# Splitting the first weight load of a decode kernel: one half row per partition ahead of four and four

## The chip, the cores and the metric

The kernel runs on one core of a Trainium2 chip. The metric is the device time of one execution in microseconds (us). A profiled execution gives, beside its time, a span: the time from the first to the last instruction that the hardware profiler recorded.

## What is computed

One token `x` of width 576 is normalised, and two branches are computed from it and added to it: attention over the last 4096 positions of a key and value cache (32 query heads on 16 key and value heads of width 128), and a gated MLP with 4608 hidden values. Cut to what matters here:

```
xn  = layernorm(x)                                   # x: 576
q   = xn @ wq                                        # wq: 576 x 4096
p   = softmax(q . k_cache[last 4096] * 128 ** -0.5)  # two query heads on each of 16 key heads
A   = (p @ v_cache[last 4096]) @ wo                  # wo: 4096 x 576
z   = gelu(xn @ w_in)                                # w_in: 576 x 4608
B   = (z[:2304] * (w_sp * layernorm(z[2304:]) + b_sp)) @ w_out
out = x + A + B
```

All inputs are bf16. The weights and the two caches together are 50.96 MB, and each byte is read once.

## The kernel before

All large transfers are issued from one queue, SyncE's (SP), in program order: the query weights `wq`, two loads of keys, the MLP's `w_in` in three loads, then keys and values by turns, the last values, `w_out`, and `wo` in four loads of 16, 10, 4 and 2 rows per partition. Each load takes one buffer of a ring of seven equal buffers (`RING = 7`, tag "ring"). A load can be issued only when what its buffer held seven loads earlier has been used; SP waits for that, and all later loads stand behind it. Each load also takes one of eight completion semaphores in turn, together with the four small transfers of ScalarE's queue, and waits until the transfer that had the semaphore before has landed.

`wq` is laid out so that partition p holds nine half rows of 2048 values (4096 B each), s = 0 to 8. `load_halves` (L76 to L81, issue on L80) loads a stretch of them for all 128 partitions in one DMA. The before kernel calls it twice for `wq`: five half rows, then four. In the trace a DMA on this queue shows as 128 packets, one for each partition (256 for keys and values, 8192 B each), spread over 16 DMA engines, and each DMA engine ends its part with a 4-byte packet for the semaphore.

ScalarE's queue carries four tiny transfers: `x64` (L110, the token on 64 partitions), `x4` (L113) and two single values (L116, L117).

The start of the computation is a chain: `x64` lands; one matmul spreads it (L174); VectorE, TensorE and GpSimd compute the mean and variance (L177 to L190); VectorE writes `XT` (L196 to L199); TensorE multiplies it with `wq` (L207: for each half row s, four matmuls of 512 columns side by side, accumulated in `qps`). Then `q_rep` (L216, L218), sixteen small matmuls (L224) and sixteen small multiplications on VectorE (L235) give `Qb`, the query operand of all heads. From there a loop goes over the 16 heads: VectorE transposes the keys (`t_head`, L247), TensorE computes the scores (`s_head`, L255), and after each group of four heads come the softmax and the product with the values (L276 to L305). The `w_in` product (L334) stands after the fourth head on TensorE. At the end TensorE multiplies with `w_out` and `wo` (L403, four matmuls a row), VectorE adds `x` (L425), and SP writes the result (L426).

Instructions of each engine run in program order (`tc.manual_schedule()`).

Of the kernel before, what the change touches and what calls it, by code (L numbers as in the profile page):

```python
# [39 lines left out]
def kernel(  # L40
# [31 lines left out]
    def ring_tile(name, rows, width):  # L72
        t = ring.tile([P, SLOT], BF16, name=name, tag="ring")
        return t[:, 0:rows * width].rearrange("p (s c) -> p s c", c=width)

    def load_halves(src, lo, n, name):  # L76

        v = ring_tile(f"{name}{lo}", n, src.shape[1] // 2)
        rows = src.rearrange("r (e c) -> (r e) c", e=2).rearrange("(p s) c -> p s c", s=NS)
        nc.sync.dma_start(v, rows[:, lo:lo + n, :])  # L80
        return [(lo + s, v[:, s, :]) for s in range(n)]  # L81
# [9 lines left out]
        return [(lo + t, v[:, t, :]) for t in range(n)]  # L91

    K, V = {}, {}
    wq_sb = load_halves(A_wq, 0, 5, "wq") + load_halves(A_wq, 5, 4, "wq")
    for m in range(2):
        K.update(load_kv(A_k_cache, m, "k"))
    win_sb = sum((load_halves(B_w_in, lo, 3, "win") for lo in (0, 3, 6)), [])
# [360 lines left out]
```

## Time and profile before

| | |
|---|---|
| median of 3 runs | 128.71 us (128.63 to 128.98) |
| the profiled execution: its time | 128.68 us |
| the profiled execution: its span | 126.9 us (1.78 us lie around it) |
| busy: TensorE matmuls, VectorE, ScalarE, GpSimd | 56%, 58%, 18%, 3% of the span |
| read from HBM | 50.96 MB, 402 GB/s over the span |
| 16 DMA engines, queue of the large loads | 95.2% of their span |
| TensorE's granted clock, mean | 0.781 |

In the timeline's lines the first two numbers are the start and the length in us, then come engine (SPq and ACTq are the DMA queues' issuing instructions), line, operation, output<-input and count, and in brackets the idle time before and what ended it. In the table of stages, "DMA share" is the time of all packets that started in the stage, as a share of 16 engines' time there (a long packet counts whole where it starts, so a short stage can show more than 1).

### The profile page before, as it was taken

Reading aid. Unit: us, or ns where it says so; the run is one execution under the profiler, and the core shown is the slowest. Engines: PE = TensorE matmul, PEld = TensorE weight load, DVE = VectorE, ACT = ScalarE, POOL = GpSimd, SP = SyncE. Lnnn points to the kernel's source line nnn. Section 1 sums busy time; section 2 is a strip of 40 time slices with the busy share of each in tenths; the row PEclk is TensorE's granted clock in tenths of the full one; section 3 lists DMA queues with packets and bytes.
Section 4 is the critical chain, followed back from the end, with each engine's and each line's share of the span. In section 5 each row is a group of like instructions: output and inputs, shape, how many; then the busy total and the mean of one; then the engine's idle time right before and its main releaser. Section 6 shows DMA issues by size and latency. Waiting matters only on the chain.

```text
span 126.9 us, 1775 instructions
## 1 busy us (share of the span) xinstructions
PE 70.5 (56%) x708; PEld 32.5 (26%) x708; DVE 74.1 (58%) x157; ACT 22.9 (18%) x76; POOL 3.6 (3%) x19
## 2 busy tenths in 40 slices
PE   0002831399999796008359456991579901862460
PEld 0002301132699621002113111231113301222350
DVE  6704145999000499455399799997999557050000
ACT  0300011000000003930000308303074039200000
POOL 3401000000000000000100000000000000000000
PEclk9999996579985559955868976999555996589755
DMA  4999999999999999999999999999999999999940
GB/s 136 433 409 429 408 429 434 444 436 418 427 413 431 418 426 429 421 431 434 421 436 423 424 436 423 429 424 421 429 431 423 431 452 442 427 418 413 415 171 0
DMA packets 5899, 51.06 MB, mean 402 GB/s; under 512 B 516, under 2 KB 516, under 8 KB 772
## 3 DMA queue, kind: packets, MB, share of 16 engines
q1 hardware_dynamic: 5800, 50.96, 95.2%
q8 instruction: 5, 0.08, 0.2%
q10 hardware_dynamic: 92, 0.00, 0.0%
q14 instruction: 2, 0.02, 0.0%
HBM read 50.96 MB, written 0.00 MB: 402 GB/s over the span
## 4 chain that ended last, share of the span: by engine, by line
issue 41%; DVE 27%; DMA 25%; PE 3%; POOLq 0%; POOL 0%
DMA wo<-in_A_wo_dram 18%; DVE kT L247 16%; DMA x<-in_A_x_dram 7%; PE out_t L403 2%; DVE mx L276 2%; DVE pt L288 2%; DVE on L319 2%; DVE om L315 1%; PE yps L322 1%; PE ps_x L184 0%; POOLq L453 0%; POOL mv L190 0%; DVE mt L265 0%; DVE lb L271 0%; DVE mb L271 0%
## 5 line engine op out<-in xcount | busy, mean ns | idle before, releaser
L255 PE MATMUL S<-kT,Qb 128*8 128x512 bf16 x128 | 40.5, 484 | 21.8 <-DVE kT L247 21.0
L247 DVE STREAM_TRANSPOSE kT<-k 128x1024 f32<-128x1024 f32 x32 | 37.0, 1211 | 10.8 <-DMA k<-in_A_k_cache_dram 10.8
L255 PEld LDWEIGHTS <-Qb 128*8 128x8 bf16 x128 | 11.7, 98 | 46.7 <-issue 38.5
L297 ACT COPY PT<-pt 32x32 f32<-32x32 f32 x64 | 15.4, 241 | 13.7 <-DVE pt L288 12.9
L281 ACT ACTIVATE p<-S,nm 128x1024 bf16<-128x1024 f32 x4 | 4.5, 1113 | 54.8 <-DVE nm L279 54.8
L305 PE MATMUL ops<-v,PT 128*8 128x512 bf16 x128 | 13.3, 453 | 0.4 <-ACT PT L297 0.4
L334 PEld LDWEIGHTS <-win 128*128 128x128 bf16 x162 | 10.1, 164 | 0.4 <-issue 0.4
L334 PE MATMUL zps<-XT,win 128*128 128x2 bf16 x162 | 10.2, 202 | 0.0
L322 PE MATMUL yps<-on,sel 128*32 128x32 f32 x32 | 2.1, 220 | 10.8 <-DVE on L319 10.8
L403 PE MATMUL out_t<-wo,Y 128*1 128x144 bf16 x128 | 3.7, 276 | 5.2 <-DMA wo<-in_A_wo_dram 5.2
L276 DVE TENSOR_REDUCE mx<-S 128x1 f32<-128x1024 f32 x4 | 4.8, 1204 | 1.6 <-PE S L255 1.6
L425 DVE TENSOR_TENSOR res<-out_t,x 97x144 bf16<-97x144 f32 x1 | 0.3, 308 | 9.1 <-PE out_t L403 9.1
L288 DVE STREAM_TRANSPOSE pt<-p 128x1024 bf16<-128x1024 bf16 x4 | 4.8, 1210 | 1.4 <-ACT p L281 1.4
L305 PEld LDWEIGHTS <-PT 128*8 128x8 bf16 x128 | 4.0, 91 | 5.8 <-issue 2.0
L174 PE MATMUL ps_x<-x,rmat 64*128 64x9 bf16 x1 | 0.2, 163 | 9.5 <-DMA x<-in_A_x_dram 9.5
L315 DVE SCALAR_TENSOR_TENSOR om<-ops,rs,dmask 128x512 f32<-128x512 f32 x4 | 3.0, 742 | 4.2 <-PE ops L305 4.2
L322 PEld LDWEIGHTS yps<-on,sel 128*32 128x32 f32 x32 | 1.7, 132 | 12.5 <-DVE on L319 10.4
L403 PEld LDWEIGHTS <-Y 128*1 128x1 bf16 x128 | 2.9, 97 | 6.0 <-issue 5.9
L207 PE MATMUL qps<-wq,XT 128*2 128x512 bf16 x36 | 3.8, 603 | 0.8 <-DVE XT L198 0.8
L319 DVE TENSOR_REDUCE on<-om 128x128 f32<-128x512 f32 x4 | 4.1, 1023 | 0.1
L218 DVE CAST q_rep<-qps 128x512 bf16<-128x512 f32 x2 | 1.4, 692 | 4.4 <-PE qps L207 3.7
L216 ACT CAST q_rep<-qps 128x512 bf16<-128x512 f32 x2 | 1.2, 585 | 14.2 <-DVE q_rep L218 14.2
(88 smaller groups left out, 35.0 us busy)
## 6 DMA issues: line engine op xcount, KB each, us to landing
k<-in_A_k_cache_dram SPq DMA_DIRECT2D x8, 2048.0 KB, 24.9
v<-in_A_v_cache_dram SPq DMA_DIRECT2D x8, 2048.0 KB, 21.7
win<-in_B_w_in_dram SPq DMA_DIRECT2D x3, 1728.0 KB, 20.6
wout<-in_B_w_out_dram SPq DMA_DIRECT2D x1, 2592.0 KB, 27.4
wq<-in_A_wq_dram SPq DMA_DIRECT2D x1, 2560.0 KB, 8.8
wo<-in_A_wo_dram SPq DMA_DIRECT2D x1, 2304.0 KB
wq<-in_A_wq_dram SPq DMA_DIRECT2D x1, 2048.0 KB, 13.0
wo<-in_A_wo_dram SPq DMA_DIRECT2D x1, 1440.0 KB
```

The costliest lines, as they stand in the source:

```text
L247: nc.vector.transpose(dst[:, 1024 * hf:1024 * (hf + 1)], src[:, 1024 * hf:1024 * (hf + 1)])
L255: nc.tensor.matmul(S[g % 2][32 * i:32 * i + 8, hf, :], lhsT=Qb[:, j, be].rearrange("p a h -> p (a h)"), rhs=kv[:, be // 2, be % 2, 16 * hf ...
L276: nc.vector.tensor_reduce(out=mx[:, 0:1], in_=s[:], op=ALU.max, axis=mybir.AxisListType.XY)
L281: nc.scalar.activation(p[:], s[:].rearrange("p a n -> p (a n)"), ACT.Exp, bias=nm[:, 0:1], scale=SCALE, accum_out=lx[:, 0:1])
L288: nc.vector.transpose(pt[:].rearrange("p t x -> p (t x)"), d["p"][:])
L297: nc.scalar.copy(PT4[32 * a:32 * a + 32, i, :], pt4[32 * i:32 * i + 32, :, a])
L305: nc.tensor.matmul(ops[32 * i:32 * i + 8, :], lhsT=d["PT"][:, i, 4 * tb:4 * tb + 4, :].rearrange("p t h -> p (t h)"), rhs=V[GK * g + i][:, ...
L315: nc.vector.scalar_tensor_tensor(out=om[:].rearrange("p c d -> p (c d)"), in0=ops[:], scalar=d["rs"][:, 0:1], in1=dmask[:].rearrange("p c ...
L319: nc.vector.reduce_sum(on[:], om[:].rearrange("p c d -> p d c"), axis=AXX)
L322: nc.tensor.matmul(yps[32 * g:32 * g + 32, :], lhsT=sel[:, dq, :], rhs=on[:, 32 * dq:32 * dq + 32], start=(dq == 0), stop=(dq == 3), tile_ ...
L334: nc.tensor.matmul(zps[:, :, t], lhsT=wt[:, t, :], rhs=XT[:, s, :], start=(s == 0 and t == 0), stop=(s == NS - 1 and t == NF - 1), skip_gr ...
L403: nc.tensor.matmul(out_t[32 * n:32 * n + 1, :], lhsT=lhs[:, col:col + 1], rhs=wv[:, CW * n:CW * (n + 1)], start=first, stop=last, tile_pos ...
```

## The change

`wq` is loaded in three DMAs of 1, 4 and 4 half rows per partition instead of two of 5 and 4. The first DMA then moves 128 x 4096 B, the second 128 x 16384 B, the third is as it was. The ring hands out one more buffer, so that the loads behind `wq` take the next buffer of the seven, and the next of the eight semaphores. The matmuls, their order and everything else in the program text are unchanged.

```diff
-    wq_sb = load_halves(A_wq, 0, 5, "wq") + load_halves(A_wq, 5, 4, "wq")
+    wq_sb = load_halves(A_wq, 0, 1, "wq") + load_halves(A_wq, 1, 4, "wq") + load_halves(A_wq, 5, 4, "wq")
```

## The prediction, made before the changed kernel was run

> **What bounds the kernel now.** I read first the slices of the page, then the chain that ended last, then the stages around the change, and last the issues of the transfers.
>
> The slices (40 of 3.17 us each), DMA engines and rate:
>
> ```profile
> DMA  4999999999999999999999999999999999999940
> GB/s 136 433 409 429 408 429 434 444 436 418 427 413 431 418 426 429 421 431 434 421 436 423 424 436 423 429 424 421 429 431 423 431 452 442 427 418 413 415 171 0
> ```
>
> From the second slice to the last but two, the DMA engines are never short of work. The chain that ended last agrees at its end:
>
> ```profile
> 98.10 23.38 DMA wo<-in_A_wo_dram
> 121.48 0.04 issue
> 121.52 1.37 PE out_t L403 x30
> ```
>
> A `wo` load issued at 98.10 lands 23.38 us later though it is 1440 KB, some 3.4 us at 430 GB/s: it stood some 20 us in the queue. After it only 5.4 us of span remain. So the time is start of the stream + bytes at the stream's rate + a fixed tail, as long as the queue never runs dry. The list of issues says that it doesn't:
>
> ```profile
> k<-in_A_k_cache_dram SPq DMA_DIRECT2D x8, 2048.0 KB, 24.9
> v<-in_A_v_cache_dram SPq DMA_DIRECT2D x8, 2048.0 KB, 21.7
> ```
>
> The third number is us from issue to landing. 2048 KB is 4.9 us at 430 GB/s, so a load typically waits 17 to 20 us behind others. The smallest of the eight `v` is 19.4 us. Compute that frees a buffer a microsecond sooner or later moves only this waiting.
>
> Now the head, where the change is (timeline):
>
> ```profile
> 0.74 0.86 SPq L80 DMA_DIRECT2D wq<-in_A_wq_dram  x2
> 1.65 1.20 SPq L85 DMA_DIRECT2D k<-in_A_k_cache_dram  x2
> 9.43 1.29 SPq L80 DMA_DIRECT2D win<-in_B_w_in_dram  x3
> 9.55 0.16 PE L174 MATMUL ps_x<-x,rmat 64*128 64x9 bf16 x1 [9.55 <-DMA x<-in_A_x_dram]
> 13.17 3.79 PE L207 MATMUL qps<-wq,XT 128*2 128x512 bf16 x36 [0.77 <-DVE XT L198]
> 17.02 0.69 DVE L218 CAST q_rep<-qps 128x512 bf16<-128x512 f32 x1 [3.72 <-PE qps L207]
> 22.90 9.13 DVE L247 STREAM_TRANSPOSE kT<-k 128x1024 f32<-128x1024 f32 x8
> 42.85 2.37 DVE L247 STREAM_TRANSPOSE kT<-k 128x1024 f32<-128x1024 f32 x2 [10.82 <-DMA k<-in_A_k_cache_dram]
> ```
>
> The token lands at 9.4 us, `XT` is ready 3.6 us later, the q matmuls end at 17.0, the first eight key transposes end at 32.0. Then VectorE waits 10.82 us for the third key load. Whatever the head gains or loses up to that size ends here.
>
> **The change, part by part.**
>
> *One more DMA in the stream.* Bytes are the same. The trace's packet records give the usual time of a packet by size: 2304 B 93 ns, 4608 B 178, 8192 B 309, 16384 B 611, 20480 B 761, 4 B 9 ns. Between 4608 and 20480 B a byte costs 583/15872 = 0.0367 ns, and 8 to 9 ns per packet are left over; a 4096 B packet is then 159 ns. A row of 20480 B (761) becomes 159 + 611 = 770 ns: +9. Each DMA engine has eight of the rows, and one more semaphore packet of 9 ns: 8 x 9 + 9 = 81 ns. All DMA engines run in parallel, so the stream ends +0.08 us later. Nothing hides this, as the stream is the bound.
>
> *The cold start.* In stages of 0.5 us (the last two numbers of a line are DMA share and GB/s):
>
> ```profile
> 1.50:2.00 0.50, 0.00 (x0) 0.00 (x0) 0.45 (x1) 0.00 (x0) 0.15 (x1) 1.00 2.06 492
> 2.00:2.50 0.50, 0.00 (x0) 0.00 (x0) 0.50 (x2) 0.00 (x0) 0.00 (x0) 1.00 0.53 123
> 2.50:3.00 0.50, 0.00 (x0) 0.00 (x0) 0.49 (x4) 0.00 (x0) 0.04 (x1) 1.00 0.09 41
> 3.00:3.50 0.50, 0.00 (x0) 0.00 (x0) 0.29 (x1) 0.48 (x1) 0.50 (x1) 1.00 1.27 532
> ```
>
> (492 + 123 + 41) x 0.5 us = 328 KB is exactly one 20480 B row on each of 16 DMA engines, and (2.06 + 0.53 + 0.09) x 0.5 = 1.34 us is its mean time, against 0.76 later: 0.58 us are start-up. The trace has no cold 4 KB row. Bounds: if the 0.58 us is a delay ahead of the first byte, the small row takes 0.74 us and nothing changes (0); if a cold first packet takes 1.34 us whatever its size, 0.60 us more is lost (1.34 - 0.74). A gain is possible only from the spread below. I take 0: second rows ran at 778 to 789 ns, nearly the usual time, so reading ahead hides the delay for all but the first, and the 2304 B packets at the end run at a steady 93 ns.
>
> *What starts earlier.* In the records `x64`'s 18-byte packets start at 5.34 us, after four `wq` rows on their DMA engine, then take turns with rows: four and a semaphore packet, ending 8.41 to 9.23 us. With 4 KB rows the same count of turns gives first packets near 3 us and landing near 4.3; if they come at 5.34 by time, five turns with 16 KB rows of 0.61 us end near 8.8. So `x` lands 0.6 to 5 us earlier, `XT` at 8 to 12.4. The second `wq` load lands where the first did (9.5), the third at 14.3 (before: issue 1.2 + 13.0 = 14.2, +0.08). Sixteen matmuls at 3.79/36 = 0.105 us stand behind the last, 1.7 us: q ends near 16.0, not 17.0. `Qb` and the first transposes start up to 1 us earlier. All of it goes into the 10.82 us wait: VectorE then waits 11.9 us for the third key load, which lands 0.08 later. Price 0; without that cover it would be -1.0.
>
> *Moved waits on SP.* The listing of the changed program against the old shows: the second key load now waits for `x64`'s semaphore (before, the first `w_in` load did), the next two for the first `wq` load and `x4`, and the third `w_in` load for the first single value and, new, for TensorE's four matmuls on half row 0, whose buffer it takes. All later loads are queued behind it on SP. Latest issue: the second key load 8.8 us, the third `w_in` load 12.8 us. Already queued then: 6.8 MB, which end at 2.4 + 15.9 = 18.3 us, and 12.4 MB, which end at 31 us. Cover 9 and 18 us, so price 0. The third key load still waits for `wq`'s matmuls: half rows 1 to 4, done before 15.5 as before. From the fourth key load on, each waits for the same work as before; the listing of TensorE, VectorE and ScalarE is the same but for one more wait (half row 1) and renumbered semaphores.
>
> *The tail* has the same loads in the same order: 0.
>
> Sum: 128.68 + 0.08 = 128.76, say 128.8 us. The profiled execution is 0.03 below the median of 128.71, far inside what a measurement of this kernel can tell from no change (0.3%, 0.39 us).
>
> The Trainium skill speaks against this change: "DMA: Bandwidth & Descriptors", Measured, asks for DMAs of 1 MiB or more, and its fit charges about 2 us for each DMA beside the bytes. The new first load has 0.5 MiB; by that rule taken at face value the sum would be near 130.8. The slices disagree: 26 loads in 122 us of steady 408 to 452 GB/s leave no room for 2 us each. No run here yet shows a small load at the head.
>
> **Rivals.**
>
> 1. *The cold start goes by packet* (slower). The first 4 KB row takes as long as the first 20 KB row, and the stream is 0.60 us behind for good: 128.76 + 0.60 = 129.4. It decides from 0.31 us of such loss on (0.39 less 0.08). For it: only one row per DMA engine moved up to 3 us. Against: the second rows' near-usual time. 0.13.
> 2. *A load's start isn't hidden* (slower). The small load is drained before the next is under way, so that a second start, issue to first packet (0.74 to 1.75 us) plus 0.58, 1.6 us, is paid: 130.4. Against: the second issue follows 0.46 us after the first, while the first row is still starting. 0.03. The skill's charge per DMA is this case.
> 3. *The earlier q counts* (faster). If the 10.82 us wait isn't the cover that I read, the 1.0 us comes through: 127.8. Against it: the queue's 17 to 20 us waits. 0.06.
> 4. *The late DMA engine shifts.* The slowest DMA engine sets the end. In the records their last packets of `wo` end between 121.3 and 123.2 us; 0.6 us of that spread is there after the first rows already (3.05 to 3.65), the rest comes from instruction fetches of 16 KB (0.9 us each) on the same engines. Shorter first rows may even out or reshuffle the 0.6: 128.2 or 129.3. 0.08 each way.
>
> That the change doesn't do what it says is out for the loads (the listing has three); that `x` isn't earlier would change nothing in the sum.
>
> **How the numbers follow.** Forecast, within 0.3%: 0.62, its own range 128.5 to 129.0 (runs of the old kernel lie within 0.35). Faster: rivals 3 and 4, 0.14. Slower: rivals 1, 2 and 4, 0.24. The range runs from the fast side of rival 4 to rival 1: 128.2 to 129.5, leaving out rivals 2 and 3.
>
> **What would show it.** Right: the first DMA packets of 4 KB at 159 ns, second rows at the usual time, 430 GB/s from 3 us on; `x` before 9 us; q matmuls in pieces, ending near 16.0; VectorE's wait for the third key load near 12 us and ending near 42.9; the last `wo` landings within 0.3 us of before. Wrong: a DMA share under 0.9 in a stage between 3 and 20 us (rivals 1, 2), the key wait gone (3), or the last `wo` landing moved by over 0.4 us with a full stream (4).

## The result, and the profile after

The changed kernel takes 128.87 us (median of 22 runs, 128.65 to 129.14) against 128.67 us of the kernel before (22 runs, 128.48 to 129.00): ratio 1.0016, 95% interval 1.0009 to 1.0022, so 0.12 to 0.28 us slower. That is within the 0.3% called no change, but it is more than the 0.08 us that the packets cost. The profiled execution took 128.82 us, with a span of 127.0 us.

The slices of the changed kernel:

```profile
DMA  4999999999999999999999999999999999999940
GB/s 84 438 434 439 400 426 428 439 427 440 440 399 423 431 416 428 428 431 431 423 426 434 423 426 434 423 423 426 428 434 423 423 467 433 409 449 399 420 180 0
```

The stream is as full as before. What differs is the first slice: 84 GB/s after 136. (Packets count where they start, and the rows started there are now small, so the drop is less than it looks.)

The issues still land some 20 us after they are made, so the queue never ran low:

```profile
k<-in_A_k_cache_dram SPq DMA_DIRECT2D x8, 2048.0 KB, 23.6
v<-in_A_v_cache_dram SPq DMA_DIRECT2D x8, 2048.0 KB, 22.0
```

The head in the timeline of the changed kernel:

```profile
0.74 1.33 SPq L80 DMA_DIRECT2D wq<-in_A_wq_dram  x3
...
4.87 0.16 PE L174 MATMUL ps_x<-x,rmat 64*128 64x9 bf16 x1 [4.87 <-DMA x<-in_A_x_dram]
5.17 5.12 SPq L80 DMA_DIRECT2D win<-in_B_w_in_dram  x3
...
9.32 2.30 PE L207 MATMUL qps<-wq,XT 128*2 128x512 bf16 x20
...
14.40 1.88 PE L207 MATMUL qps<-wq,XT 128*2 128x512 bf16 x16 [2.78 <-DMA wq<-in_A_wq_dram]
...
16.32 0.69 DVE L218 CAST q_rep<-qps 128x512 bf16<-128x512 f32 x1 [6.74 <-PE qps L207]
```

The token lands at 4.9 us instead of 9.4, the q matmuls run in two pieces, and q is done at 16.3 instead of 17.0. The 0.7 us won goes where the prediction sent it, VectorE's wait for the third key load (VectorE's timeline):

```profile
22.22 9.12 DVE L247 STREAM_TRANSPOSE kT<-k 128x1024 f32<-128x1024 f32 x8
42.76 2.37 DVE L247 STREAM_TRANSPOSE kT<-k 128x1024 f32<-128x1024 f32 x2 [11.42 <-DMA k<-in_A_k_cache_dram]
```

11.42 us of waiting instead of 10.82, ending within 0.1 us of where it ended. The chain that ended last goes through a `wo` load again, now the last of the four (before, the second, issued at 98.10):

```profile
101.51 22.13 DMA wo<-in_A_wo_dram
123.68 0.44 PE out_t L403 x8
124.14 0.31 DVE res L425
```

In the packet records the last `wo` packet ends at 123.18 us before and 123.32 now. The mean of the 16 DMA engines' ends, which is steadier than the last one, goes from 121.91 to 122.07 us.

The cold start in stages of 0.5 us (last two numbers: DMA share, GB/s):

```profile
1.50:2.00 0.50, 0.00 (x0) 0.00 (x0) 0.45 (x1) 0.00 (x0) 0.15 (x1) 1.00 0.99 90
2.00:2.50 0.50, 0.00 (x0) 0.00 (x0) 0.50 (x2) 0.00 (x0) 0.00 (x0) 1.00 0.64 106
2.50:3.00 0.50, 0.00 (x0) 0.00 (x0) 0.50 (x4) 0.00 (x0) 0.03 (x1) 1.00 0.72 213
3.00:3.50 0.50, 0.00 (x0) 0.00 (x0) 0.29 (x1) 0.49 (x1) 0.50 (x1) 1.00 0.94 360
```

(90 + 106 + 213) x 0.5 us = 205 KB started by 3 us are three rows of 4 KB on each of 16 DMA engines, in (0.99 + 0.64 + 0.72) x 0.5 = 1.2 us. In the running stream, three such rows take 3 x 0.159 = 0.48 us. So not only the first small row is slow. In the packet records 38 of the 128 small rows take over 15 ns longer than usual, the slowest 1.15 us.

To compare heads I add up, over the packets of the large loads in the first 7 us, the time beyond the usual one of their size (those over by more than 15 ns), and divide by 16. This start-up loss is 0.61 us for each DMA engine before and 0.76 in the changed kernel.

### The profile page after: what moved, and what is told of

Read it like the earlier page. It is cut to its first block, busy times and chain, and to the rows that moved or that the text cites. A ratio compares the mean times of both kernels' runs of the same rounds, so it can differ in the third digit from the quotient of the medians.

```text
span 127.0 us, 1776 instructions
## 1 busy us (share of the span) xinstructions
PE 70.9 (56%) x708; PEld 32.6 (26%) x708; DVE 74.1 (58%) x157; ACT 22.9 (18%) x76; POOL 3.7 (3%) x19
## 4 chain that ended last, share of the span: by engine, by line
issue 44%; DVE 28%; DMA 17%; PE 7%; POOLq 0%; POOL 0%; SPq 0%
DMA wo<-in_A_wo_dram 17%; DVE kT L247 14%; PE S L255 4%; DVE mx L276 2%; DVE pt L288 2%; DVE on L319 2%; DVE S L159 1%; PE ops L305 1%; DVE om L315 1%; PE yps L322 1%; POOLq L453 0%; PE ps_x L184 0%; POOL mv L190 0%; DVE ops L162 0%; DVE qps L133 0%
## 5 line engine op out<-in xcount | busy, mean ns | idle before, releaser
L235 DVE TENSOR_SCALAR Qb<-qps,mask 128x32 bf16<-128x32 f32 x16 | 2.7, 349 | 1.3 <-PE qps L224 1.3
```

## Experiments

The theory after the result: 0.08 us for eight packets and a semaphore packet on each DMA engine, and some 0.1 us because the small load is the first. The rivals: any load more costs 0.2 us wherever it stands; the head's chain counts after all; 0.08 is all and the rest chance. Changes below are against the kernel before if nothing else is said, and the edits are shown shortened. A stream that already runs is called warm, its start cold.

**Small loads behind the old first one** (e1).

```diff
-load_halves(A_wq, 0, 5, "wq") + load_halves(A_wq, 5, 4, "wq")
+load_halves(A_wq, 0, 5, "wq") + four loads of 1
```

> wq in five loads of 5, 1, 1, 1 and 1 half rows: three loads more than before, all behind the old first load, so that the stream starts as before. Theory (a split costs its packets and semaphores, 4 x 159 - 611 = 25 ns on each of 8 rows and 3 x 9 ns, and what the change lost beyond its 0.08 us is the cold start): +0.23 us, first rows and the time to 3 us as before. Rival (every additional load costs the 0.20 us that the change measured, wherever it stands): +0.6 us.

Measured 1.0037 (1.0024 to 1.0050), +0.48 us (0.31 to 0.64). In its profile the mean end of the DMA engines is 122.14, +0.23 us as worked out, and the start-up loss is 0.53 us, no more than before. But the time is clearly above 0.23, and 0.6 is inside the interval. By its time alone this run speaks for the rival. In the profiled execution the latest DMA engine accounts for part of the excess: the last `wo` packet ends at 123.49 us, 0.31 later than in the profile before, and the time, 129.04 us, is 0.36 longer.

**The same three loads in other orders** (e2, e10, e11).

```diff
-1, 4, 4
+4, 1, 4   (e2, e10)      4, 4, 1   (e11)
```

> The same three loads in the order 4, 1, 4: the small one runs in a warm stream, the first rows have 16 KB. Theory (cold start): +0.08 us against the kernel before; each DMA engine ends wq 0.08 us later than before, not 0.25 as in the changed kernel. Rival (the additional load costs 0.20 us wherever it stands): +0.20 us, and wq ends 0.25 us later here too.

> 4, 1, 4 again. Theory: +0.08 us against the kernel before. Rival (the order doesn't matter): as 1, 4, 4 in this set, +0.2 us or more.

> 4, 4, 1: the small load is the last of the three. Theory: +0.08 us against the kernel before, as 4, 1, 4. Rival (the order doesn't matter): as 1, 4, 4 in this set.

Measured: 1.0005 (0.9997 to 1.0014), 1.0005 (0.9993 to 1.0016) and 0.9998 (0.9988 to 1.0009). Weighted by their intervals that is +0.04 us, about -0.04 to 0.11: the 0.08 us of the packets fits, 0.20 us for a load more does not.

**The change again** (e8, e9).

> The changed kernel once more, on the same chip as the runs with 1, 1, 1, 2, 4 and with small w_in packets, for a second profile of its head. Theory: +0.2 us, the DMA engines end wq on average 0.15 to 0.2 us later than before and the stream as much later. Rival (0.08 us is all that there is, the rest was chance): +0.08 us, and wq ends 0.08 us later.

> The changed kernel (1, 4, 4) beside the same three loads in other orders, on one chip. Theory (0.08 us for packets, and some 0.1 us or more for the small load being the first): +0.2 to +0.35 us. Rival (the order doesn't matter): the same time as 4, 1, 4 and 4, 4, 1 within 0.05 us.

Measured 1.0031 (1.0019 to 1.0043) and 1.0007 (0.9997 to 1.0016). In the second set the interval reaches both theories; that set alone does not separate the orders. With the 22 runs of the result, weighted in the same way, the change costs +0.21 us, about 0.14 to 0.27. Against the three other orders the difference is 0.17 us, about 0.07 to 0.27 (taken as independent, though runs of one set share the runs of the kernel before). So among these three loads the place of the small one counts.

The packet records separate the orders more clearly. The mean time at which the 16 DMA engines end the last `wq` load (their semaphore packets) is 13.75, 13.92 and 13.83 us in the three profiles of the change, 13.66, 13.60 and 13.59 in the other orders, and 13.59 to 13.67, mean 13.63, in the five profiles with two `wq` loads (before, e4, e6, e7, e12). So the change is 0.2 us late when `wq` ends, and the other orders, whose packets are the same, are on average not late; e8 alone, at 0.33 us after the kernel before, missed its expected 0.15 to 0.2. The lateness stays to the end: the mean ends of the stream are 122.07, 122.24 and 122.15 us with the change and 121.98, 122.01 and 121.99 with the other orders, 0.16 us apart.

One view points the same way: the rate from 1.5 to 10 us, by which time all these kernels are in rows of 16 KB. Before; changed; 4, 1, 4:

```profile
1.50:10.00 8.50, 0.16 (x1) 0.10 (x1) 3.96 (x11) 1.28 (x1) 1.70 (x11) 1.00 0.99 394
```

```profile
1.50:10.00 8.50, 1.52 (x12) 1.01 (x16) 5.78 (x23) 1.28 (x1) 2.27 (x12) 1.00 0.98 378
```

```profile
1.50:10.00 8.50, 0.75 (x3) 0.70 (x4) 4.29 (x14) 1.28 (x1) 1.70 (x11) 1.00 0.99 390
```

The last numbers are GB/s. The two further profiles of the change have 372 and 376, 4, 4, 1 has 392 and the other profile of 4, 1, 4 has 386. 16 GB/s over 8.5 us are 136 KB, 0.3 us of stream; the figure is coarse, since a packet counts whole: e4, whose loads are those of the kernel before, has 384. The start-up loss is finer. Nine profiles whose first rows are of 16 or 20 KB (before, e1, e2, e4, e6, e7, e10, e11, e12) have 0.52 to 0.74 us, mean 0.61. Four whose first load is one half row in 4 KB packets (after, e5, e8, e9) have 0.67 to 0.84, mean 0.74. Single profiles overlap; the means differ by 0.13 us, and 0.13 + 0.08 = 0.21 us is what the change costs. The changed kernel with 1 KB packets (e3, below) is in neither group.

**Two loads, 4 and 5** (e12).

> Two loads as before, but 4 half rows first and then 5: the same packets in another order, first rows of 16 KB instead of 20 KB. Theory: 0. Rival (the size of the first rows counts in proportion, 4 KB less of 16 KB less): a quarter of what 1, 4, 4 loses beyond 0.08 us, +0.03 to 0.07 us.

Measured 0.9998 (0.9986 to 1.0010): first rows of 16 KB do as well as 20 KB, within 0.18 us.

**Small loads at the head** (e5: 1, 1, 1, 2, 4).

> wq in five loads as in the run with 5, 1, 1, 1, 1, but with the small ones at the head: 1, 1, 1, 2, 4. By the packets' times the same work: (3 x 159 + 309 - 761) x 8 + 3 x 9 = 0.23 us. Theory (cold start): the head loses some 0.1 us more, so that the 16 DMA engines end the stream on average 0.3 to 0.4 us later than before, against 0.23 us in the run with the small loads behind; time +0.35 us or more. Rival (the place doesn't matter): average end +0.23 us, time as in that run, +0.5 us.

Measured 1.0033 (1.0021 to 1.0045), +0.42 us (0.27 to 0.58): the theory's 0.35 is inside, but the run with the small loads behind is as slow, and the mean end, 122.13, is only 0.22 us later than before. The expected average end of 0.3 to 0.4 us was missed. `wq` ends at 13.78 us on average, 0.15 after the 13.63 of two loads, and at 13.82 in the run with the small loads behind: neither is later than its packets' 0.23. So with five loads the place made no difference that these runs show.

**Still smaller packets at the head** (e3).

```diff
 first wq load of the changed kernel:
-v = buffer[:, 0:2048]                            # 128 packets of 4096 B
+v = buffer[:, 0:4*520] as (4, 520)[:, :, 0:512]  # 512 packets of 1024 B
```

> The changed kernel (1, 4, 4) with its first half row in packets of 1024 B instead of 4096 B (four pieces a little apart in the buffer, still one load). Four packets of some 46 ns instead of one of 159 cost 25 ns on each of 8 rows, 0.20 us, in a warm stream. Theory A (a cold DMA engine moves a few packets, whatever their size, until the first answers are there): the cold phase moves a quarter of the bytes, some 6 KB less for each engine, +0.2 us more, +0.6 us in all against the kernel before. Theory B (the cold start is a delay of fixed length and the changed kernel's loss beyond 0.08 us has another cause): +0.20 us over the changed kernel, +0.4 us in all, and the cold phase no longer than there.

Measured 1.0030 (1.0018 to 1.0042), +0.39 us (0.23 to 0.54). Theory A's 0.6 is out. A 1024 B packet takes 46 ns as expected, and the start-up loss is 0.59 us, not more than with large rows, though the first packet starts 0.08 us later. So a cold DMA engine is not limited to a few packets whatever their size. `wq` ends at 13.83 us on average, 0.20 after the 13.63 of two loads, where the packets alone were worked out at 0.28: here, too, nothing is lost beyond the packets.

**XT late** (e4: six VectorE writes ahead of the mean; they cost more than planned).

> The kernel before with six VectorE writes of 128x1024 values (0.91 us each, the outcome is not used) between the token's arrival and XT: q is some 5.5 us later. Theory (all that the head gains or loses goes into VectorE's 10.8 us wait for the third key load): time unchanged within 0.1 us, that wait falls to 5 to 6 us. Rival (the head's chain counts): +5.5 us, or a part of it.

VectorE's timeline of this run (line numbers are 3 higher):

```profile
19.89 0.23 DVE L202 TENSOR_SCALAR XT<-xn,mask 128x4 bf16<-128x4 f32 x1
...
42.29 2.37 DVE L250 STREAM_TRANSPOSE kT<-k 128x1024 f32<-128x1024 f32 x2 [3.17 <-DMA k<-in_A_k_cache_dram]
```

`XT` is ready 7 us later than before, the wait falls from 10.82 to 3.17 us, and it ends at 42.3. The time: 1.0009 (1.0000 to 1.0018), +0.12 us and at most 0.23 for a delay of 7 us. The head's compute has 7 us of cover at least; the 0.7 us that the change gains there is well inside it.

**More loads without smaller packets** (e6), **smaller packets without more loads** (e7).

```diff
 e6, load_kv, into the same buffer:
-nc.sync.dma_start(v, both heads)
+for h in range(2): nc.sync.dma_start(v[:, h, :], head h)
 e7, load_halves, w_in alone:
-v = buffer as (3, 2304)
+v = buffer as (3, 2368)[:, :, 0:2304]
```

> The kernel before with each of its 16 loads of keys and values issued as two DMAs, one for each head, into the same buffer: 16 loads more, the same 8192 B packets, one more 4 B packet of 9 ns on each DMA engine for each load. Theory (a load more costs its semaphore packet and no more): +0.14 us. Rival (a load as such costs 0.12 to 0.16 us beyond its packets, as the run with five loads of wq would have it if its 0.48 us were all real): +2 us or more.

> The kernel before with its three w_in loads in packets of 4608 B instead of 13824 B (the three half rows of a partition stand a little apart in the buffer): no load more, 48 packets more on each DMA engine, (3 x 178 - 516) x 8 x 3 = 0.43 us. Theory (the stream is the bound and a packet more costs 9 ns there): +0.43 us. Rival (packets cost nothing at the end of the stream, the loads do): 0. Other rival (small packets cost double of what their records say): +0.9 us.

Measured e6: 1.0032 (1.0020 to 1.0044), +0.41 us (0.26 to 0.57) for 16 loads, 0.026 us each. The rival's 2 us is out. The excess over 0.14 isn't in the stream: over its five runs 2.11 us lie outside the span on average, in the 17 runs of the kernel before 1.81, and the span itself is 126.90 us against 126.78. So 0.12 us are within the span, as the theory has it, and 0.30 us outside; what takes them there isn't shown. Its page against that of the kernel before:

```profile
DMA packets 6155, 51.06 MB, mean 402 GB/s; under 512 B 772, under 2 KB 772, under 8 KB 1028
```

```profile
DMA packets 5899, 51.06 MB, mean 402 GB/s; under 512 B 516, under 2 KB 516, under 8 KB 772
```

The 256 packets more are semaphore packets, 16 for each of 16 loads. Measured e7: 1.0023 (1.0014 to 1.0032), +0.30 us (0.18 to 0.41), against 0.43 by the records: packets do cost time at the end of the stream, rather less than their records say (0.30 / 48 = 6 ns each, not 9), not double.

## Why the prediction was right

The forecast, no change within 0.3%, at 128.8 us, held; the median is 128.87, and the range holds it. The mechanism, a full stream and a covered head, held too. The sum did not quite: the measured 0.12 to 0.28 us is more than its 0.08, and the forecast held all the same because what it left out is small beside 0.39 us.

- *What bounds the kernel* held: the stream is full from the second slice on in every run, and 7 us of delay in the head moved the time by 0.23 us at most.
- *One more DMA*, +0.08 us: the packet records of the changed kernel have 159 ns for 4096 B and 611 for 16384 B, as worked out, and where the small load is not the first the measured cost is 0.04 us (-0.04 to 0.11).
- *The cold start*, taken as 0, is the term that was mis-sized: for 1, 4, 4 it is 0.13 us by the start-up loss, inside the bounds of 0 and 0.60. I leaned on the second rows' near-usual time and on the steady 2304 B packets at the end. The first was a reading of 20 KB rows, the second of a warm stream; neither is a small row at the start, of which several in a row were slow.
- *Rival 1*, the same loss at 0.60 us, decided nothing: it needed 0.31 us. Its mechanism, a cold packet that takes as long whatever its size, was refuted by the rows themselves: the 90 x 0.5 us = 45 KB started by 2 us are eleven small rows, in 0.99 x 0.5 x 16 / 11 = 0.72 us each on average, not 1.34. The packets of 1 KB speak against it too.
- *Rival 2*, a second start for the small load, 1.6 us, did not happen. The Trainium skill's rule ("DMA: Bandwidth & Descriptors": 1 MiB or more for a DMA in Measured, and in the section on the anatomy of one DMA a fixed 2 us for each, both measured on DMAs that GpSimd issues) does not hold as a sum for loads queued behind others: sixteen loads more cost 0.41 us, not 32.
- *Rival 3*, the earlier q: refuted by e4. The gain was 0.7 us rather than 1.0, since q ended at 16.3, not near 16.0.
- *Rival 4*, the late DMA engine: the ends of the engines in the changed profile spread from 121.43 to 123.32 us, as wide as before, and the last end moved by 0.14 us, no more than the mean end, so no shift shows there. But the last end differs from profile to profile (in e8's it is 123.89, and that execution took 129.41 us). This limits what a single profile can show here, and a small shift of the late engine is not ruled out.
- *What starts earlier*: the token landed at 4.9 us, within the bounds. Its packets came at 3.7 us, once a DMA engine had ended the whole first load, not after four rows. `XT` then waited for VectorE, still busy with its opening writes until 5.7 us.
- *Moved waits on SP* and *the tail*, both 0, held: SP did wait for the matmuls on half row 0, as read from the listing, but issued the third `w_in` load at 9.96 us, earlier than the 12.8 allowed for, and the queue stayed full to the `wo` loads.

Open: why 1, 4, 4 starts up more slowly than 4, 1, 4 and 4, 4, 1, while 1, 1, 1, 2, 4 and 1 KB packets lose nothing beyond their packets by the end of `wq`. So small first rows as such are not shown to be the cause; what is shown is that the order of these three loads counts. Open is also how much of the 0.25 us by which e1's time is above its packets is the latest DMA engine, beyond the one profiled execution.

## What to carry to other kernels

In a kernel bound by one full transfer queue, work that starts earlier is worth nothing until a wait on the queue is gone: find the next wait for a transfer behind the change (here 10.8 us) before counting a gain. Price a split by its packets, here 6 to 9 ns each on a DMA engine, and not by loads. The order of the first loads can cost more than that: 1, 4, 4 ended its stream 0.16 us later than 4, 1, 4 and 4, 4, 1. A small load is worth trying behind a large one, but no rule against small first loads follows, since 1, 1, 1, 2, 4 lost nothing beyond its packets.

## What was not expected of the hardware

- The start of the stream costs each DMA engine about 0.61 us beyond its packets' usual times with rows of 16 or 20 KB first, 0.74 us with 4 KB rows first (four profiles, one of them no later at the end of `wq` than its packets make it), and 0.59 us with 1 KB packets first (one profile).
- `x64`'s packets took turns with 20 KB rows from the fifth row on before (from 5.3 us), but with a 4 KB first load they all passed in a row behind it (3.7 us).
- Instruction fetches (five packets of 16 KB in each profile, 0.88 to 0.97 us each) share the DMA engines with the loads: while one runs, the records show packets of the loads on 15 engines instead of 16, in all 14 profiles.
- The time follows the latest DMA engine: in all 14 profiles the span is 3.6 to 3.9 us longer than its last `wo` packet's end, which lies between 123.02 and 123.90 us. That the fetches decide which engine is the latest is not shown.
